# Scaling the weights instead of the activations in the opening of an attention and MLP kernel, with the warm-up dummies rearranged

## The chip, the cores and the metric

One core of one Trainium2 chip. The metric is device time in microseconds (us) per execution, the median of several executions; each comes with the core's span (first to last instruction, about 1.7 us shorter in most executions) and the mean clock that the TensorE throttle granted. The engines are named as in the profile: PE is TensorE, PEld its weight loads, DVE VectorE, ACT ScalarE, POOL GpSimd, SP SyncE, which issues DMAs.

## The reference, cut to what matters

```python
x = A_x                                                   # 2048 x 512
sa, ca, ga, sb, cb, gb = silu(c) @ w_mod, cut in six      # shift, scale, gate, twice
h = layernorm(x) * (1 + ca) + sa
q = h @ wq                                                # 32 heads of 128
x = x + ga * (softmax(q k^T / sqrt(128)) v @ wo)          # 512 keys, 8 kv heads
h = layernorm(x) * (1 + cb) + sb
x = x + gb * (relu(h @ w1) @ w2)
```

The change rests on one identity. With n = layernorm(x), h @ wq = n @ ((1 + ca) wq) + sa @ wq: the scale can go into the rows of the weights, and the shift becomes a bias per column of q.

## The kernel before

The work is cut into 128 units (4 blocks of 512 rows times 32 heads). For each unit PE makes the projection q, the scores, and the product with v; ACT takes the exponentials and evacuates q; DVE divides. The main loop is dense on PE. Before it stands an opening of 13 us that loads, normalizes and transposes the first 512 rows, makes the modulation columns modc (shift and scale, one column per 128 features), and projects q for units 0 and 1 in two halves of 256 rows. Bank 4 (QBK) holds unit 0's first half, then unit 1's second half, then the projection of unit 2.

```python
warm(7); silu_exp(5); warm(9)        # dummies 128x512; silu_exp transposes c on PE
...                                   # statistics, rstd on POOL, normalized x (xn)
ln_tposes(0, TB[0])                   # tile 0 of xn, transposed by PE into PSUM
for f in mod_cols_mm(0, QBK): f()     # 32 matmuls of one column: modc
ln_norm(2)
mod_cols_evac(0, QBK)
for tl in range(1, TPB):
    ln_tposes(tl, TB[tl // 2])
mod_half(0, 0, DVE); mod_half(0, 2, ACT); mod_half(0, 1, DVE); mod_half(0, 3, ACT)   # h out of PSUM
q_half(0, 0, CC_ORDER, QBK)           # 4 matmuls, stationary wq, moving h, 256 columns
mod_half(1, 0, DVE); mod_half(1, 2, ACT); mod_half(1, 1, DVE); mod_half(1, 3, DVE)
q_evac_half(0, 0, QBK, ACT)
q_half(1, 0, CC_ORDER, 5);  q_evac_half(1, 0, 5, ACT)
q_half(0, 1, CC_ORDER, 6);  q_evac_half(0, 1, 6, DVE)
q_half(1, 1, CC_ORDER, QBK); q_evac_half(1, 1, QBK, DVE)
...
for s in range(NU):                   # main loop
    s_mms(s, 0)
    q_mms(s + QA)                     # QA = 2: the first is unit 2's projection, into QBK
    s_mms(s, 1)
    ...
```

Each operation names the resources it reads and writes; a helper turns them into semaphore waits. Two operations that write resources of one name wait for each other even where their memory is disjoint.

Of the kernel before, what the change touches and what calls it, by code (L numbers as in the profile page):

```python
# [8 lines left out]
ACTF = mybir.ActivationFunctionType  # L9
ALU = mybir.AluOpType  # L10
AX = mybir.AxisListType
BF = mybir.dt.bfloat16
F32 = mybir.dt.float32
# [1185 lines left out]
def build_fast(nc, es, top, A_x, A_k_cache, A_v_cache, A_wq, A_wo, B_x, B_w1, B_w2, c, w_mod, out, flag):  # L1199
    P = 128  # L1200
    _, Sq, D = A_x.shape
    _, G, Sk, Dh = A_k_cache.shape
# [5 lines left out]
    QB = 512  # L1208
    NB = Sq // QB
    TPB = QB // P  # L1210
    NT = Sq // P
    DC = D // P
# [3 lines left out]
    scale = float(Dh) ** -0.5  # L1216
# [11 lines left out]
    def T(name, shape, dt=BF):  # L1228
        return es.enter_context(nc.sbuf_tensor(name, shape, dt))
# [3 lines left out]
    wq_sb = wq_t[:, :].rearrange("p (c n) -> p c n", c=DC)  # L1233
# [4 lines left out]
    hT = [T(f"hT{i}", [P, DC, QB]) for i in range(2)]  # L1238
    h2T = [T(f"h2T{i}", [P, DC, QB]) for i in range(2)]
    qT = [T(f"qT{i}", [P, QB]) for i in range(NQT)]  # L1240
    PT = [T(f"PT{i}", [P, KC, QB]) for i in range(NPT)]
# [8 lines left out]
    xn = T("xn", [P, TPB, D])  # L1250
    xnT = T("xnT", [P, TPB, DC, P])
# [4 lines left out]
    ones = T("ones", [P, P])  # L1256
# [7 lines left out]
    modc = T("modc", [P, 4 * DC], F32)  # L1264
# [5 lines left out]
    mv = T("mv", [P, NT, 2], F32)  # L1270
    rstd = T("rstd", [P, NT], F32)
    cst = T("cst", [P, 4], F32)
    rinv = T("rinv", [P, NU, TPB], F32)
    vmax = T("vmax", [P, 2, G], F32)
    chk = T("chk", [P, 12], F32)
# [6 lines left out]
    bank = [s_ps[0][:, 0, :], s_ps[0][:, 1, :], s_ps[1][:, 0, :], s_ps[1][:, 1, :], q_ps[:, :],  # L1282
            o_ps[:, 0:2, :].rearrange("p a b -> p (a b)"), o_ps[:, 2:4, :].rearrange("p a b -> p (a b)"), w_ps[:, :]]
    QBK, WBK = 4, 7

    sem = lambda name: top.enter_context(nc.semaphore(name))
    kb = KB(nc)
    PE = kb.stream("pe", sem("s_pe"))
    ACT = kb.stream("act", sem("s_act"))
    DVE = kb.stream("dve", sem("s_dve"))  # L1290
    POOL = kb.stream("pool", sem("s_pool"))
# [7 lines left out]
    def dma(out_ap, in_ap, key, reads=(), writes=(), transpose=False, eng=None):  # L1299
        k = dsem(key)  # L1300
        if transpose:
            return kb.op(SP, lambda e: e.dma_start_transpose(out_ap, in_ap), reads=reads, writes=writes, dma_sem=k)
        return kb.op(eng or SP, lambda e: e.dma_start(out_ap, in_ap), reads=reads, writes=writes, dma_sem=k)  # L1303

    RL = lambda name, n: [Res(f"{name}{i}") for i in range(n)]
    R_x, R_wq, R_wo = RL("x", NT), RL("wq", H), RL("wo", NPASS)
    R_kT, R_v, R_v1 = RL("kT", G), RL("v", G), Res("v1")
    R_hT, R_h2T = [RL(f"hT{i}_", DC) for i in range(2)], [RL(f"h2T{i}_", DC) for i in range(2)]
    R_qT, R_PT, R_o, R_oT = RL("qT", NQT), [RL(f"PT{i}_", 2) for i in range(NPT)], RL("o", NOS), RL("oT", NOT)
# [3 lines left out]
    R_b = RL("bank", 8)  # L1313
# [1 line left out]
    R_moda, R_modb, R_ga, R_gb = Res("moda"), Res("modb"), Res("ga"), Res("gb")  # L1315
    R_pr = [R_ga] + RL("pr", 2) + [R_gb]
    R_st, R_mv, R_rstd = RL("st", NT), RL("mv", NT), RL("rstd", NT)
    R_h0 = RL("h0", DC)
    R_q1 = RL("q1_", 2)
    R_cf, R_m01 = Res("cf"), Res("m01")  # L1320
    R_s3, R_eps = Res("s3"), Res("eps")
# [49 lines left out]
    def mm(out_ap, lhsT, rhs, start, stop, reads, bk, signal):  # L1371
        kb.op(PE, lambda e: e.matmul(out_ap, lhsT, rhs, start=start, stop=stop), reads=reads, group_writes=[R_b[k] for k in bk], signal=signal)  # L1372
# [4 lines left out]
    def warm(n):  # L1377
        for i in range(n):
            mm(bank[WBK], ones[:, :], ones[:, 0:1].to_broadcast([P, QB]), True, True, [R_ones], [WBK], i == n - 1)
# [11 lines left out]
    def ln_norm(t):  # L1391
        b, tl = t // TPB, t % TPB
        kb.op(DVE, lambda e: e.tensor_scalar(xn[:, tl, :], x_sb[:, t, :], mv[:, t, 0:1], rstd[:, t:t + 1], op0=ALU.subtract, op1=ALU.mult),
              reads=[R_x[t], R_mv[t], R_rstd[t]], writes=[R_xn[tl]])

    def ln_dmaT():
        dma(xnT[:, :, :, :].rearrange("p t c q -> p (t c) q"), xn[:, :, :].rearrange("p t d -> p (t d)"), "xnT", reads=R_xn, writes=[R_xnT], transpose=True)

    def ln_mod_sb(cc, dst, R_dst, which):
        o, r = (0, R_moda) if which == 1 else (2 * DC, R_modb)  # L1400
# [4 lines left out]
    def ln_tposes(tl, bks):  # L1405
        for cc in range(DC):
            bk = bks[cc]
            o = (cc % 2) * 512 + tl * P
            tpose(bank[bk].bitcast(BF)[:, o:o + P], xn[:, tl, cc * P:(cc + 1) * P], [R_xn[tl]], [bk], cc == DC - 1)

    CC_ORDER = (0, 2, 1, 3)
    QA = 2

    def silu_exp(bk):
        cT = bank[bk].bitcast(BF)[:, 0:DC]
        kb.op(PE, lambda e: e.transpose(cT, c_row[:, :], ident[0:DC, 0:DC]), reads=[R_c, R_ident], group_writes=[R_b[bk]])  # L1416
        kb.op(ACT, lambda e: e.activation(tmp[:, :], cT, ACTF.Exp, scale=-1.0), reads=[R_b[bk]], writes=[R_tmp])
        kb.op(ACT, lambda e: e.activation(c_f[:, :], cT, ACTF.Copy), reads=[R_b[bk]], writes=[R_cf])
# [6 lines left out]
    def mod_cols_mm(which, bk):  # L1425
        fs = []
        for cc in range(DC):
            for sl in (0, 1):
                for c2 in range(DC):
                    last = sl == 1 and c2 == DC - 1 and cc == DC - 1  # L1430
                    fs.append(lambda sl=sl, c2=c2, cc=cc, col=sl * DC + c2, last=last: mm(
                        bank[bk][:, col:col + 1], wm[sl][:, cc, c2 * P:(c2 + 1) * P], sc_bf[:, cc:cc + 1],
                        cc == 0 and sl == 0 and c2 == 0, last, [R_sc, wm_res(sl, cc)], [bk], last))
        return fs

    def mod_cols_evac(which, bk):
        mo, r = which * 2 * DC, (R_moda, R_modb)[which]
        kb.op(DVE, lambda e: e.tensor_tensor(modc[:, mo:mo + 2 * DC], bank[bk][:, :2 * DC], m01[:, :], op=ALU.add), reads=[R_b[bk], R_m01], writes=[r])  # L1438
# [38 lines left out]
    def q_mms(u, bk=QBK):  # L1477
        b, h = units[u]
        for i, cc in enumerate(range(DC)):
            mm(bank[bk], wq_sb[:, cc, h * Dh:(h + 1) * Dh], hT[b % 2][:, cc, :], i == 0, i == DC - 1,  # L1480
               [R_wq[h], R_hT[b % 2][cc]] + ([R_h0[cc]] if b == 0 else []), [bk], i == DC - 1)
        q_evac(u, bk)

    def q_evac(u, bk=QBK):
# [80 lines left out]
    load_wq(2, 2)  # L1565
    load_k(0)
    load_v(0)
    kb.op(POOL, lambda e: e.memset(ones[:, :], 1.0), writes=[R_ones])
    kb.op(POOL, lambda e: e.memset(cst[:, 0:1], -0.5), writes=[R_cst])
    kb.op(POOL, lambda e: e.affine_select(ident[:, :], ones[:, :], pattern=[[1, P]], compare_op=ALU.is_equal, fill=0.0,  # L1570
                                          base=0, channel_multiplier=-1), reads=[R_ones], writes=[R_ident])
# [3 lines left out]
    kb.op(POOL, lambda e: e.memset(m01[:, 0:DC], 0.0), writes=[R_m01])  # L1575
    kb.op(POOL, lambda e: e.memset(m01[:, DC:2 * DC], 1.0), writes=[R_m01])
    kb.op(ACT, lambda e: e.activation(cst[:, 2:3], cst[:, 0:1], ACTF.Exp), reads=[R_cst], writes=[Res("dummy")])
    warm(7)
    silu_exp(5)
    warm(9)  # L1580
    t3 = TPB - 1
    kb.op(ACT, lambda e: e.activation(xn[:, t3, :], x_sb[:, t3, :], ACTF.Copy, accum_out=s3[:, 0:1]), reads=[R_x[t3]], writes=[R_xn[t3], R_s3])
    kb.op(ACT, lambda e: e.activation(s3[:, 1:2], s3[:, 0:1], ACTF.Copy, scale=-1.0 / D), reads=[R_s3], writes=[R_s3])
# [6 lines left out]
    def rstd_pow(lo, hi):  # L1590
# [12 lines left out]
    ln_norm(1)  # L1603
    kb.op(POOL, lambda e: e.tensor_scalar(xn[:, t3, :], x_sb[:, t3, :], s3[:, 1:2], rstd[:, t3:t3 + 1], op0=ALU.add, op1=ALU.mult),
          reads=[R_x[t3], R_rstd[t3], R_s3], writes=[R_xn[t3]])
    TB = [[0, 0, 2, 2], [1, 1, 3, 7]]
    def q_evac_half(u, hf, bk, eng):
        src, dst = bank[bk][:, hf * HB:(hf + 1) * HB], qT[u][:, hf * HB:(hf + 1) * HB]
        w = [R_q1[u]] if hf else [R_qT[u]]
        if eng is DVE:  # L1610
            kb.op(DVE, lambda e: e.tensor_copy(dst, src), reads=[R_b[bk]], writes=w)  # L1611
        else:
            kb.op(ACT, lambda e: e.activation(dst, src, ACTF.Copy), reads=[R_b[bk]], writes=w)

    ln_tposes(0, TB[0])
    fs = mod_cols_mm(0, QBK)
    for f in fs:
        f()
    ln_norm(2)
    mod_cols_evac(0, QBK)  # L1620
    HB = QB // 2
    R_half = [R_h0, R_hT[0]]

    def mod_half(hf, cc, eng):
        bk = TB[hf][cc]
        o = (cc % 2) * 512 + hf * HB
        src, dst = bank[bk].bitcast(BF)[:, o:o + HB], hT[0][:, cc, hf * HB:(hf + 1) * HB]
        sc, sh = modc[:, DC + cc:DC + cc + 1], modc[:, cc:cc + 1]
        if eng is DVE:
            kb.op(DVE, lambda e: e.tensor_scalar(dst, src, sc, sh, op0=ALU.mult, op1=ALU.add), reads=[R_b[bk], R_moda], writes=[R_half[hf][cc]])  # L1630
        else:
            kb.op(ACT, lambda e: e.activation(dst, src, ACTF.Identity, bias=sh, scale=sc), reads=[R_b[bk], R_moda], writes=[R_half[hf][cc]])

    def q_half(u, hf, order, bk):
        for cc in order:
            mm(bank[bk][:, hf * HB:(hf + 1) * HB], wq_sb[:, cc, u * Dh:(u + 1) * Dh], hT[0][:, cc, hf * HB:(hf + 1) * HB], cc == CC_ORDER[0], cc == CC_ORDER[-1],
               [R_wq[u], R_half[hf][cc]], [bk], cc == CC_ORDER[-1])

    for tl in range(1, TPB):
        ln_tposes(tl, TB[tl // 2])  # L1640
    mod_half(0, 0, DVE)
    mod_half(0, 2, ACT)
    mod_half(0, 1, DVE)
    mod_half(0, 3, ACT)
    q_half(0, 0, CC_ORDER, QBK)
    mod_half(1, 0, DVE)
    mod_half(1, 2, ACT)
    mod_half(1, 1, DVE)
    mod_half(1, 3, DVE)
    q_evac_half(0, 0, QBK, ACT)  # L1650
    q_half(1, 0, CC_ORDER, 5)
    q_evac_half(1, 0, 5, ACT)
    q_half(0, 1, CC_ORDER, 6)
    q_evac_half(0, 1, 6, DVE)
    q_half(1, 1, CC_ORDER, QBK)
    q_evac_half(1, 1, QBK, DVE)
    load_wq(R, R)
    load_k(1)
# [234 lines left out]
```

## Time and profile before

| | before |
|---|---|
| time, median of the first three executions | 560.62 us (560.35 to 561.12) |
| span of the profiled execution (561.1 us) | 559.4 us |
| PE busy | 98% |
| start of unit 2's projection in that profile | 13.56 us |

The profiled execution was the slowest of the three.

The prediction shows the lines that carry the reading. Four more, from the timeline of DVE, belong to the part that the change rewrites (start us, length us, engine, line, operation, out<-in, count): five modulations out of PSUM, the last of them among the projections, then two evacuations back to back and nothing between them.

```profile
10.30 1.36 DVE L1630 TENSOR_SCALAR hT<-psS,modc 128x256 bf16<-128x256 bf16 x4
11.59 0.40 DVE L1630 TENSOR_SCALAR hT<-psW,modc 128x256 bf16<-128x256 bf16 x1
12.55 0.43 DVE L1611 CAST qT<-psO 128x256 bf16<-128x256 f32 x1 [0.57 <-PE psO L1372]
12.99 0.42 DVE L1611 CAST qT<-psQ 128x256 bf16<-128x256 f32 x1
```

The second evacuation ends at 13.41, and unit 2's projection, which overwrites what it read, starts 0.15 later.

### The profile page before, as it was taken

The page shows a single profiled execution, that of the slowest core. Times are in us where ns is not written, and L with a number is a line of the kernel's source. Part 1 is how long each engine was busy: PE and PEld are TensorE (multiplying, and loading weights), DVE is VectorE, ACT ScalarE, POOL GpSimd, SP SyncE. Part 2 cuts the span into 40 slices and gives each one's busy share as a digit, 9 for nine tenths or more (in the row PEclk, how much of TensorE's full clock was granted, in tenths as well). Part 3 has the DMA queues.
Part 4 walks back from the last instruction along what each step waited for, and adds up shares of the span by engine and source line. Part 5 has one row for each costly group of instructions (what it writes and reads, how often), then busy time and mean ns, then how long its engine had stood idle before and what let it go on. Part 6 is the DMA issues. An engine that isn't in the chain of part 4 may idle for free.

```text
span 559.4 us, 9666 instructions
## 1 busy us (share of the span) xinstructions
PE 550.5 (98%) x4060; PEld 315.8 (56%) x4134; DVE 253.8 (45%) x551; ACT 348.9 (62%) x453; POOL 54.7 (10%) x53
## 2 busy tenths in 40 slices
PE   8999999999999999999999999999999999999998
PEld 4665555555555555555555555555555654444444
DVE  4455555553546544335445443333354448321134
ACT  4986666666666666666666666666666644432500
POOL 3000022004410000033000000332000000000000
DMA  9897763513114144352352412111215110210001
GB/s 268 248 207 174 143 169 46 114 39 76 40 38 76 39 73 117 58 133 57 94 95 57 76 40 39 39 39 38 39 39 76 39 30 0 44 34 23 22 29 47
DMA packets 113309, 42.67 MB, mean 76 GB/s; under 512 B 93928, under 2 KB 112104, under 8 KB 113256
## 3 DMA queue, kind: packets, MB, share of 16 engines
q1 hardware_dynamic: 112024, 40.82, 34.3%
q10 hardware_dynamic: 1232, 1.15, 0.6%
q8 instruction: 33, 0.54, 0.4%
q14 instruction: 20, 0.16, 0.1%
HBM read 18.35 MB, written 2.10 MB: 37 GB/s over the span
## 4 chain that ended last, share of the span: by engine, by line
PE 98%; issue 1%; DMA 1%; DVE 0%; SPq 0%; DVEq 0%
PE psS L1372 28%; PE psO L1372 27%; PE psQ L1372 23%; PE psW L1372 20%; DMA c_row<-in_c_dram 1%; DVE qT L1611 0%; DVE hT L1630 0%; SPq L1303 0%; DVE PT L1723 0%; DVE PT L1725 0%; PE psS L1375 0%; PE psO L1416 0%; DVE modc L1438 0%; DVEq L123 0%
## 5 line engine op out<-in xcount | busy, mean ns | idle before, releaser
L1493 ACT ACTIVATE PT<-psS 128x1024 bf16<-128x1024 f32 x256 | 262.7, 1028 | 128.2 <-PE psS L1372 128.1
L1372 PE MATMUL psS<-qT,kT 128*128 128x512 bf16 x508 | 150.9, 379 | 0.5 <-DVE qT L1611 0.4
L1372 PEld LDWEIGHTS psO<-v,PT 128*128 128x128 bf16 x2048 | 126.6, 98 | 30.2
L1372 PE MATMUL psO<-v,PT 128*128 128x129 bf16 x2048 | 137.0, 220 | 0.0
L1372 PE MATMUL psQ<-hT,wq 128*128 128x512 bf16 (+1 forms) x510 | 130.5, 377 | 0.3 <-DVE hT L1630 0.2
L1503 DVE RECIPROCAL rinv<-psO 128x4 f32<-128x4 f32 x128 | 23.3, 182 | 227.2 <-PE psO L1372 227.2
L1372 PE MATMUL psW<-wo,oT 128*128 128x512 bf16 x454 | 118.1, 379 | 3.0
L1504 DVE TENSOR_TENSOR o<-psO,rinv 128x512 bf16<-128x512 f32 x128 | 88.5, 691 | 4.9 <-DVE rinv L1503 0.5
L1372 PEld LDWEIGHTS psQ<-hT,wq 128*128 128x128 bf16 x512 | 49.9, 98 | 60.3 <-issue 0.6
L1372 PEld LDWEIGHTS psS<-qT,kT 128*128 128x128 bf16 x512 | 49.5, 98 | 58.9 <-ACT PT L1493 0.7
L1485 ACT ACTIVATE qT<-psQ 128x512 bf16<-128x512 f32 x126 | 74.7, 593 | 0.0
L1712 ACT ACTIVATE wq<-psS 128x512 bf16<-128x512 f32 x56 | 33.4, 597 | 49.3 <-PE psS L1372 48.9
L1372 PEld LDWEIGHTS psW<-wo,oT 128*128 128x128 bf16 x512 | 45.0, 98 | 32.9 <-DVE acc L1526 1.2
L1526 DVE TENSOR_TENSOR acc<-psW,acc 128x512 f32<-128x512 f32 x48 | 33.2, 691 | 6.5 <-PE psW L1372 6.5
L1372 PE MATMUL psO<-wmw,wq 128*128 128x512 bf16 (+1 forms) x165 | 32.8, 352 | 0.3
L1529 POOL TENSOR_TENSOR acc<-acc,gaf 128x512 f32<-128x512 f32 x12 | 15.6, 1303 | 146.7 <-DVE acc L1526 139.8
L1388 POOL TENSOR_TENSOR rstd<-rstd,cst 128x4 f32<-128x4 f32 x7 | 7.2, 1025 | 216.8 <-DVE rstd L1387 216.8
L1723 DVE TENSOR_TENSOR PT<-psO,gbf 128x512 f32<-128x512 f32 (+1 forms) x12 | 7.5, 624 | 40.4 <-PE psO L1372 40.4
L1372 PE MATMUL psS<-h2T,wmw 128*128 128x512 bf16 x109 | 25.0, 379 | 0.2
L1372 PEld LDWEIGHTS psO<-wmw,wq 128*128 128x128 bf16 x168 | 15.3, 98 | 16.5
L1372 PE MATMUL psS<-hT,wmw 128*128 128x512 bf16 x110 | 24.4, 379 | 0.1
L1382 DVE BATCH_NORM_STATS2 st<-x 128x6 f32<-128x512 bf16 x31 | 21.1, 681 | 4.8 <-DMA x<-in_A_x_dram 4.8
(85 smaller groups left out, 192.6 us busy)
## 6 DMA issues: line engine op xcount, KB each, us to landing
wo<-in_A_wo_dram SPq DMA_DIRECT2D x4, 1024.0 KB, 5.9
wq<-in_A_wq_dram SPq DMA_DIRECT2D x7, 512.0 KB, 4.6
wmw<-in_B_w_dram SPq DMA_DIRECT2D x14, 256.0 KB, 3.1
wmw<-in_w_mod_dram SPq DMA_DIRECT2D x5, 512.0 KB, 4.8
oT<-o SPq DMA_TRANSPOSE x128, 2.4
out_dram<-PT SPq DMA_DIRECT2D x15, 128.0 KB, 1.7
x<-in_A_x_dram SPq DMA_DIRECT2D x3, 512.0 KB, 4.3
v<-in_A_v_cache_dram SPq DMA_DIRECT2D x8, 128.0 KB, 3.8
```

The lines of the kernel that those rows point to most:

```text
L1372: kb.op(PE, lambda e: e.matmul(out_ap, lhsT, rhs, start=start, stop=stop), reads=reads, group_writes=[R_b[k] for k in bk], signal=signal)
L1382: kb.op(DVE, lambda e: e.bn_stats(st[:, t, :], x_sb[:, t, :]), reads=[R_x[t]], writes=[R_st[t]])
L1388: kb.op(POOL, lambda e: e.tensor_tensor(rstd[:, sl], rstd[:, sl], cst[:, 0:1].to_broadcast([P, hi - lo]), op=ALU.pow), reads=R_rstd[sl] + ...
L1485: kb.op(ACT, lambda e: e.activation(qT[u % NQT][:, :], bank[bk], ACTF.Copy), reads=[R_b[bk]], writes=[R_qT[u % NQT]])
L1493: kb.op(ACT, lambda e: e.activation(PT[u % NPT][:, pr * 2:pr * 2 + 2, :], s_ps[pr][:, :, :], ACTF.Exp, scale=scale), reads=[R_b[pr * 2], R ...
L1503: kb.op(DVE, lambda e: e.reciprocal(rinv[:, u, :], o_ps[:, :, P]), reads=[R_b[5], R_b[6]], writes=[R_rinv])
L1504: kb.op(DVE, lambda e: e.tensor_tensor(o_sb[u % NOS][:, :, :], o_ps[:, :, 0:P], rinv[:, u, :].unsqueeze(2).to_broadcast([P, TPB, P]), op=A ...
L1526: kb.op(DVE, lambda e: e.tensor_tensor(acc[:, tl, :], bank[WBK], acc[:, tl, :], op=ALU.add), reads=[R_b[WBK], R_acc[tl]], writes=[R_acc[tl]])
L1529: kb.op(eng, lambda e: e.tensor_tensor(acc[:, tl, :], acc[:, tl, :], gaf[:, :], op=ALU.mult), reads=[R_acc[tl], R_ga], writes=[R_acc[tl]])
L1712: kb.op(ACT, lambda e: e.activation(h1T[b % 2][:, fc, :], bank[bk], ACTF.Relu), reads=[R_b[bk]], writes=[R_h1[b % 2][fc]], pre=all_events( ...
L1723: kb.op(DVE, lambda e: e.tensor_tensor(yt[i][:, c0:c1], bank[bk][:, c0:c1], gbf[:, c0:c1], op=ALU.mult), reads=[R_b[bk], R_gb], writes=[R_ ...
```

## The change

Its intent: the first projections need not wait for a modulated h. Plain normalized x is copied out of PSUM while the modulation is still being computed; modc then scales 256 weight columns; the shift enters as a bias at the evacuation of q. The dummies are rearranged so that PE has no idle time between them. h itself is still needed from unit 2 on, and is now made later, from the copied x.

```diff
-    kb.op(POOL, lambda e: e.memset(ones[:, :], 1.0), writes=[R_ones])
+    kb.op(DVE, lambda e: e.memset(ones[:, :], 1.0), writes=[R_ones])
-    warm(7)
-    silu_exp(5)
-    warm(9)
+    warm(10)
+    silu_exp(5)
+    warm(7)
...
+    wqs = PT[2][:, :, 0:2 * Dh]                            # scaled weights, in a buffer still free
+    R_wqs = [R_PT[2][cc // 2] for cc in range(DC)]
...
     ln_tposes(0, TB[0])
+    ln_tposes(1, TB[0])
     (modulation matmuls)
     ln_norm(2)
+    x_evac(0, 1, DVE, 2)                                   # plain x, PSUM to SBUF
     mod_cols_evac(0, QBK)
-    (eight mod_half, woven among the projections)
+    x_evac(0, 0, ACT, 0)
+    (transposes of tiles 2 and 3)
+    for cc in range(DC):                                   # DVE: weights times (1 + ca)
+        wqs[:, cc, :] = wq_sb[:, cc, 0:256] * modc[:, DC + cc]
+    (POOL: shift to bf16; PE: 8 one-column matmuls; ACT: qb, the bias)
+    q_half(0, 0, QBK);  q_half(1, 0, 5)
+    x_evac(1, 0, ACT, 1);  x_evac(1, 1, DVE, 3)
+    q_evac_half(0, 0, QBK, ACT);  q_evac_half(1, 0, 5, ACT)   # now adding qb
+    q_half(0, 1, 6);  q_half(1, 1, QBK)
+    h_mod(3, POOL);  h_mod(0, DVE)                         # h for units 2 and later
+    q_evac_half(0, 1, 6, DVE)
+    h_mod(1, DVE);  h_mod(2, DVE)
+    q_evac_half(1, 1, QBK, DVE)
```

(Lines in parentheses and the wqs line are shortened; cuts are marked with dots.)

More of the change, by code (lines that the diff above doesn't have):

```diff
@@ L1272, in build_fast @@
     cst = T("cst", [P, 4], F32)
+    sh_bf = T("sh_bf", [P, DC])
+    qb = T("qb", [P, 2], F32)
+    wqs = PT[2][:, :, 0:2 * Dh]
     rinv = T("rinv", [P, NU, TPB], F32)
@@ L1317, in build_fast @@
     R_st, R_mv, R_rstd = RL("st", NT), RL("mv", NT), RL("rstd", NT)
-    R_h0 = RL("h0", DC)
+    R_xh = [RL(f"xh{i}_", 2) for i in range(2)]
+    R_sh, R_qb = Res("sh"), Res("qb")
+    R_wqs = [R_PT[2][cc // 2] for cc in range(DC)]
     R_q1 = RL("q1_", 2)
@@ L1396, in ln_dmaT @@
     def ln_dmaT():
-        dma(xnT[:, :, :, :].rearrange("p t c q -> p (t c) q"), xn[:, :, :].rearrange("p t d -> p (t d)"), "xnT", reads=R_xn, writes=[R_xnT], transpose=True)
+        dma(xnT[:, :, :, :].rearrange("p t c q -> p (t c) q"), xn[:, :, :].rearrange("p t d -> p (t d)"), "xnT", reads=R_xn, writes=[R_xnT] + R_xh[0] + R_xh[1], transpose=True)
     def ln_mod_sb(cc, dst, R_dst, which):
@@ L1409, in ln_tposes @@
             tpose(bank[bk].bitcast(BF)[:, o:o + P], xn[:, tl, cc * P:(cc + 1) * P], [R_xn[tl]], [bk], cc == DC - 1)
-    CC_ORDER = (0, 2, 1, 3)
     QA = 2
@@ L1480, in q_mms @@
             mm(bank[bk], wq_sb[:, cc, h * Dh:(h + 1) * Dh], hT[b % 2][:, cc, :], i == 0, i == DC - 1,
-               [R_wq[h], R_hT[b % 2][cc]] + ([R_h0[cc]] if b == 0 else []), [bk], i == DC - 1)
+               [R_wq[h], R_hT[b % 2][cc]], [bk], i == DC - 1)
         q_evac(u, bk)
@@ L1605, in build_fast @@
           reads=[R_x[t3], R_rstd[t3], R_s3], writes=[R_xn[t3]])
-    TB = [[0, 0, 2, 2], [1, 1, 3, 7]]
+    TB = [[0, 0, 2, 2], [1, 1, 3, 3]]
     def q_evac_half(u, hf, bk, eng):
@@ L1610, in q_evac_half, with x_evac @@
         if eng is DVE:
-            kb.op(DVE, lambda e: e.tensor_copy(dst, src), reads=[R_b[bk]], writes=w)
+            kb.op(DVE, lambda e: e.tensor_scalar(dst, src, qb[:, u:u + 1], None, op0=ALU.add), reads=[R_b[bk], R_qb], writes=w)
         else:
-            kb.op(ACT, lambda e: e.activation(dst, src, ACTF.Copy), reads=[R_b[bk]], writes=w)
+            kb.op(ACT, lambda e: e.activation(dst, src, ACTF.Identity, bias=qb[:, u:u + 1]), reads=[R_b[bk], R_qb], writes=w)
+    HB = QB // 2
+    HT = TPB // 2
+    def x_evac(hf, j, eng, bk):
+        src = bank[bk].bitcast(BF).rearrange("p (c t q) -> p c t q", c=2, t=TPB)[:, :, hf * HT:(hf + 1) * HT, :]
+        dst = xnT[:, hf * HT:(hf + 1) * HT, 2 * j:2 * j + 2, :].rearrange("p t c q -> p c t q")
+        if eng is DVE:
+            kb.op(DVE, lambda e: e.tensor_copy(dst, src), reads=[R_b[bk]], writes=[R_xh[hf][j]])
+        else:
+            kb.op(ACT, lambda e: e.activation(dst, src, ACTF.Copy), reads=[R_b[bk]], writes=[R_xh[hf][j]])
     ln_tposes(0, TB[0])
+    ln_tposes(1, TB[0])
     fs = mod_cols_mm(0, QBK)
@@ L1619, in build_fast @@
     ln_norm(2)
+    x_evac(0, 1, DVE, 2)
     mod_cols_evac(0, QBK)
-    HB = QB // 2
-    R_half = [R_h0, R_hT[0]]
-    def mod_half(hf, cc, eng):
-        bk = TB[hf][cc]
-        o = (cc % 2) * 512 + hf * HB
-        src, dst = bank[bk].bitcast(BF)[:, o:o + HB], hT[0][:, cc, hf * HB:(hf + 1) * HB]
-        sc, sh = modc[:, DC + cc:DC + cc + 1], modc[:, cc:cc + 1]
-        if eng is DVE:
-            kb.op(DVE, lambda e: e.tensor_scalar(dst, src, sc, sh, op0=ALU.mult, op1=ALU.add), reads=[R_b[bk], R_moda], writes=[R_half[hf][cc]])
-        else:
-            kb.op(ACT, lambda e: e.activation(dst, src, ACTF.Identity, bias=sh, scale=sc), reads=[R_b[bk], R_moda], writes=[R_half[hf][cc]])
@@ L1634, in q_half @@
-    def q_half(u, hf, order, bk):
-        for cc in order:
-            mm(bank[bk][:, hf * HB:(hf + 1) * HB], wq_sb[:, cc, u * Dh:(u + 1) * Dh], hT[0][:, cc, hf * HB:(hf + 1) * HB], cc == CC_ORDER[0], cc == CC_ORDER[-1],
-               [R_wq[u], R_half[hf][cc]], [bk], cc == CC_ORDER[-1])
-    for tl in range(1, TPB):
-        ln_tposes(tl, TB[tl // 2])
-    mod_half(0, 0, DVE)
-    mod_half(0, 2, ACT)
-    mod_half(0, 1, DVE)
-    mod_half(0, 3, ACT)
-    q_half(0, 0, CC_ORDER, QBK)
-    mod_half(1, 0, DVE)
@@ L1647, in build_fast, with q_half @@
-    mod_half(1, 2, ACT)
-    mod_half(1, 1, DVE)
-    mod_half(1, 3, DVE)
+    x_evac(0, 0, ACT, 0)
+    def q_half(u, hf, bk):
+        for cc in range(DC):
+            mm(bank[bk][:, hf * HB:(hf + 1) * HB], wqs[:, cc, u * Dh:(u + 1) * Dh], xnT[:, hf * HT:(hf + 1) * HT, cc, :], cc == 0, cc == DC - 1,
+               [R_wqs[cc], R_xh[hf][cc // 2]], [bk], cc == DC - 1)
+    for tl in range(2, TPB):
+        ln_tposes(tl, TB[tl // 2])
+    for cc in range(DC):
+        kb.op(DVE, lambda e, cc=cc: e.tensor_scalar(wqs[:, cc, :], wq_sb[:, cc, 0:QA * Dh], modc[:, DC + cc:DC + cc + 1], None, op0=ALU.mult),
+              reads=[R_wq[0], R_wq[1], R_moda], writes=[R_wqs[cc]])
@@ new lines, in build_fast @@
+    kb.op(POOL, lambda e: e.tensor_copy(sh_bf[:, :], modc[:, 0:DC]), reads=[R_moda], writes=[R_sh])
+    for u in range(QA):
+        for cc in range(DC):
+            mm(bank[WBK][:, u:u + 1], wq_sb[:, cc, u * Dh:(u + 1) * Dh], sh_bf[:, cc:cc + 1], cc == 0, cc == DC - 1, [R_wq[u], R_sh], [WBK], u == QA - 1 and cc == DC - 1)
+    q_half(0, 0, QBK)
+    q_half(1, 0, 5)
+    x_evac(1, 0, ACT, 1)
+    x_evac(1, 1, DVE, 3)
+    kb.op(ACT, lambda e: e.activation(qb[:, :], bank[WBK][:, 0:QA], ACTF.Copy), reads=[R_b[WBK]], writes=[R_qb])
@@ L1650, in build_fast, with h_mod @@
     q_evac_half(0, 0, QBK, ACT)
-    q_half(1, 0, CC_ORDER, 5)
     q_evac_half(1, 0, 5, ACT)
-    q_half(0, 1, CC_ORDER, 6)
+    q_half(0, 1, 6)
+    q_half(1, 1, QBK)
+    def h_mod(cc, eng):
+        kb.op(eng, lambda e: e.tensor_scalar(hT[0][:, cc, :].rearrange("p (t q) -> p t q", t=TPB), xnT[:, :, cc, :], modc[:, DC + cc:DC + cc + 1],
+                                             modc[:, cc:cc + 1], op0=ALU.mult, op1=ALU.add),
+              reads=[R_xh[0][cc // 2], R_xh[1][cc // 2], R_moda], writes=[R_hT[0][cc]])
@@ L1654, in build_fast @@
+    h_mod(3, POOL)
+    h_mod(0, DVE)
     q_evac_half(0, 1, 6, DVE)
-    q_half(1, 1, CC_ORDER, QBK)
+    h_mod(1, DVE)
+    h_mod(2, DVE)
     q_evac_half(1, 1, QBK, DVE)
```

## The prediction

> **What bounds the kernel now.** I read the page first (part 1, busy time; part 4, the chain that ended last), then the chain of waits in order of time for the opening, then the timeline of the first 16 us engine by engine, and last the waits of PE alone. Of the page two lines matter:
>
> ```profile
> PE 550.5 (98%) x4060; PEld 315.8 (56%) x4134; DVE 253.8 (45%) x551; ACT 348.9 (62%) x453; POOL 54.7 (10%) x53
> PE 98%; issue 1%; DMA 1%; DVE 0%; SPq 0%; DVEq 0%
> ```
>
> PE is busy 98% of 559.4 us and carries 98% of the chain that ended last. So work removed from another engine is worth nothing once PE runs densely; only the moment at which PE starts to run densely counts, plus any hole made later. PE's own waits over the whole run are four, all in the first 14 us:
>
> ```profile
> PE psW L1372 <- POOL cst L1569: 1.0, 1, 1.0
> PE psO L1416 <- DMA c_row<-in_c_dram: 0.7, 1, 0.7
> PE psS L1372 <- DVE qT L1611: 0.4, 1, 0.4
> PE psQ L1372 <- DVE hT L1630: 0.2, 1, 0.2
> ```
>
> The change touches nothing outside this opening. Its chain reads so (start us, us, what):
>
> ```profile
> 1.24 3.66 DMA c_row<-in_c_dram
> 5.13 3.86 PE psW L1372 x9
> 8.98 0.22 PE psS L1375 x4
> 9.21 0.79 PE psQ L1372 x32
> 10.02 0.18 DVE modc L1438
> 10.30 0.42 DVE hT L1630
> 10.86 0.78 PE psQ L1372 x4
> 12.55 0.44 DVE qT L1611
> 13.34 0.38 PE psS L1372
> 13.72 0.87 PE psQ L1372 x4
> ```
>
> The nine psW matmuls are dummies; then x's transposes, the 32 modulation matmuls, the modulation columns modc, the modulated h, four half query projections, their evacuation, the first scores (a record is missing: the weight load at 13.10 puts their true start at 13.12), and from 13.56 the projection of unit 2. From there PE is dense to the end: 10.61 of 10.90 us busy from 13.10 to 24, 198.5 of 200 from 100 to 300. **The number to follow is therefore the start of unit 2's projection, 13.56 us;** what it moves by, the end moves by.
>
> [...] the dummies are 0.43 us apart (nine in 3.86) while later 128x512 matmuls are 0.215 apart (four in 0.86), the seven early dummies end near 4.05, PE idles until 4.95, and full speed comes only near 8.8, in the last dummy. [...] 128x512 from SBUF takes 0.406 us, 128x256 from PSUM 0.401. [...] The one POOL normalization (0.90 us, 8.70 to 9.60) overlaps a DVE one, so the trace shows no clear block; I keep 0.90.
>
> **The change, part by part.** Hand-offs as in the trace of before: DVE or POOL to PE 0.15 us, PE to DVE or ACT 0.04 after the matmul's end, DVE to itself 0.1 where it waits for its own result; steps of DVE 0.32 for 128x512 from SBUF (0.406 latency), by the same fixed part about 0.2 for 128x256 (0.27 latency, an estimate), 0.61 for 128x512 from PSUM (0.69 latency as L1524; less if a bf16 copy is faster).
>
> *Dummies.* Before: 7, the transpose of c, then 9. After: 10, the transpose, then 7, with the ones set by DVE instead of POOL (PE starts near 0.95 instead of 1.04). Ten cold dummies end at 0.95 + 10 x 0.427 = 5.22, while c has landed at 4.90. So the transpose of c, silu on POOL, the reciprocal square root queued behind it on POOL and the normalizations all slip by D = 5.23 - 4.94 = 0.29 us; D is 0 if the clock opens before 5.2. [...]
>
> *Front end.* The first normalized tile is ready at 7.82 + 0.41 = 8.23 + D, the second at 8.56 + D. Before, PE was in dummies until 8.82, so the gain here is real. But the change puts the second tile's transposes ahead of the modulation matmuls: these begin at 8.56 + 0.15 + 0.22 = 8.93 + D, against 9.04, run 0.8, and modc starts at 9.94 + D (before 10.02) and ends at 10.11 + D. With D = 0.29 that is 0.2 later than before.
>
> *From modc to the projections.* Removed: eight 128x256 modulations out of PSUM (five DVE, three ACT). Added ahead of the projections: four DVE scalings of weights, 128x256: from 10.22 + D, ready at 10.49, 10.68, 10.87, 11.06 + D; the bias chain (POOL copy of the shift 0.2, eight one-column matmuls at 0.025, one ACT copy 0.2), which lets PE into the projections at 10.76 + D. The fourth scaling rules: the first half projection streams its last matmul from 11.21 to 11.32 + D, the next three (4 x 0.109 each) end streaming at 11.76, 12.20 and 12.64 + D. The four evacuations of plain x are beside this: two lie before modc, and the later two (ACT done near 11.0 + D, DVE near 11.67 + D) come in time. Before, the projections streamed from 10.86 to 12.79. So weights instead of activations gain nothing here: same number of matmuls, one DVE chain of four in front of them.
>
> *After the projections.* Hidden before, because h was the product itself; new now: h for units 2 and later must still be made, one 128x512 on POOL (0.9, beside) and three on DVE, woven among the evacuations. DVE: h0; evacuation of unit 0's second half, 12.40 to 12.83 + D (before 12.55 to 12.98); h1; h2; evacuation of unit 1's second half. The first scores start at 12.98 + D, before 13.12. But unit 2's projection writes the bank that the last evacuation reads, and that one now stands behind two 128x512 operations: 12.75, 13.08, 13.41 + D, done 13.83 + D, PE on at **13.98 + D, against 13.56**. PE has two score matmuls (0.43) to fill the time from 12.98 and stands 0.57 us.
>
> Sum: +0.42 + D. ACT takes back a little (its first exponential comes earlier): the next projection waits for ACT at 15.68 + D against 15.32, so **+0.36 + D: 0.36 to 0.65 us later, about 0.6**[...].
>
> Against that stands the clock. [...] The timed runs, 560.35 to 561.12, spread by 0.77[...]. I put the mean loss of before beyond its profile at 0.3 us, and the change takes that loss away. Net: +0.6 - 0.3 = +0.3 us.
>
> **Rivals.** (a) *The clock rules*: the hole is gone, PE is warm in every run, and the change wins 0.5 to 1 us: 559.8. For it: the spread above, and "kept dense" as its stated aim. Against: the profile of before was warm by the first real matmul, and it is no faster than the other runs. (b) *DVE rules*: the weight scalings, the PSUM copies and h on one engine delay the last evacuation, as computed[...]: 561.5 to 562. For it: DVE has twelve operations between about 9.1 + D and 13.8 + D; against: its operations there are short. (c) *Hidden anyway*: the delay of unit 2 is refilled since ACT is nearly as loaded as PE in the first units (10.02 of 10.90 us busy from 13.10 to 24). Against: PE has no idle there either, so nothing refills it. It would give 560.6.
>
> **Range and chances.** 560.62 + 0.3 = 560.9. Low end 560.1, where D is 0 and the clock gains 0.8; high end 561.8, where D is 0.29, the clock gains nothing[...]. Two per cent is 11 us, and the whole opening lasts 13: 1% for faster, 98% for within 2%, 1% for slower.
>
> **What would show it.** In the changed profile: ten dummies without a hole and the transpose of c at about 5.2 (4.94 before); full-speed dummies among the last seven, then PE idle before the first transposes near 8.6; modc near 10.2; first scores near 13.2; a new wait of PE, psQ on DVE qT, of about 0.5 us just before unit 2's projection at about 14.2. Wrong would be: a projection of unit 2 before 13.6 (DVE faster than I take it, or D zero); no early full speed in the dense dummies[...]; or h3 on POOL as what PE waits for.

The forecast's sum came to +0.6 - 0.3 = +0.3 us, so 560.9, with a range of 560.1 to 561.8. Passages are cut, as marked, in which the author reasoned from rules that no trace of this case shows: when the clock opens, what a late opening would cost, and that POOL and DVE can hold each other up. No cut changes the sum. The 0.3 is the author's estimate, with only the spread of three executions, 0.77 us, beside it. The upper end, 561.8, and the 561.5 to 562 of rival (b) still contain the cut term for POOL and DVE, about 0.5 us of the upper end.

## The result, and the profile after

| | before | after |
|---|---|---|
| median | 560.46 us | 562.81 us |
| lowest to highest, 6 executions each | 560.09 to 561.12 | 562.31 to 563.14 |
| ratio, with 95% interval | | 1.0040 (1.0027 to 1.0053) |

A ratio is the mean time of one kernel's fast executions over that of the other's of the same rounds, so it is not quite the ratio of the medians. The change costs 2.3 us: same by the 2% rule, clearly slower by the interval, and outside the predicted range.

The page of the changed kernel has a row that the page of before did not have (that trace holds no clock record): PEclk, the granted clock in tenths over 40 slices of 14 us each.

```profile
PEclk8999999999999999999999999999999999999999
```

The 8 in the first slice says that the clock was cut in the opening. Stretches of 4 us show where (stretch, length, busy time and count of PE, PEld, DVE, ACT, POOL, then granted clock, DMA share and GB/s):

```profile
8.00:12.00 4.00, 3.39 (x62) 2.60 (x63) 3.28 (x11) 1.31 (x4) 2.01 (x4) 0.90 1.25 267
12.00:16.00 4.00, 3.53 (x17) 1.95 (x17) 1.60 (x5) 1.82 (x3) 0.55 (x1) 0.67 1.15 326
```

The clock record in the trace gives it exactly: opened at 4.38 us, halved at 11.20, open again at 14.62 (in a later trace, e7: 4.06, 10.89, 14.30). One warning: five of the 17 kept traces (before, e3, e5, e12, e13) hold no clock record at all, and a run without a record is listed with a clock of 1.0. A listed 1.0 alone doesn't prove that the clock stayed open; there the spacing of the matmuls has to show it. Nor does a late opening show in the listed mean: it reads 1.0 for the profiled execution of e1, whose dummies ran at 0.427 us each until the clock opened at 8.80. The chain of waits, in order of time (short steps of issue are left out here and below), shows what the halving does:

```profile
8.31 0.72 PE psS L1380 x8
9.03 0.79 PE psQ L1377 x32
9.84 0.18 DVE modc L1442
10.12 0.30 DVE PT L1647
10.44 0.49 DVE PT L1647 x2
10.96 0.30 DVE PT L1647
11.31 0.61 PE psQ L1377 x2
11.91 1.72 PE psO L1377 x8
13.66 0.48 DVE qT L1615
14.14 0.65 DVE hT L1664 x2
14.79 0.39 DVE qT L1615
15.33 1.02 PE psQ L1377 x4
```

The eight psO matmuls take 1.72 us; before they took 0.89. Ahead of them stand four weight scalings (PT) that are not back to back: the second and the fourth start only when the one before is complete. Behind them stand two h operations between the two evacuations. Unit 2's projection, the number that the prediction follows, starts at 15.33 instead of 13.56. PE's waits name the idle time after the dummies, which was not there in the profile before:

```profile
PE psS L1380 <- DVE xn L1398: 1.5, 1, 1.5
PE psQ L1377 <- DVE sc_f L1677: 0.3, 1, 0.3
```

The last line names sc_f, a tiny operation that follows the last evacuation on DVE; the evacuation, which ends at 15.18, is what PE needs.

### The profile page after: what moved, and what is told of

Read it like the earlier page. It is cut to its first block, busy times and chain, and to the rows that moved or that the text cites. A ratio compares the mean times of both kernels' runs of the same rounds, so it can differ in the third digit from the quotient of the medians.

```text
span 561.3 us, 9692 instructions
## 1 busy us (share of the span) xinstructions
PE 551.1 (98%) x4069; PEld 316.4 (56%) x4143; DVE 255.2 (45%) x556; ACT 349.0 (62%) x453; POOL 55.7 (10%) x54
## 4 chain that ended last, share of the span: by engine, by line
PE 97%; issue 1%; DVE 1%; POOL 0%; ACT 0%; DVEq 0%; POOLq 0%
PE psS L1377 28%; PE psO L1377 27%; PE psQ L1377 23%; PE psW L1377 20%; DVE PT L1647 0%; POOL tmp L1426 0%; DVE qT L1615 0%; PE psS L1380 0%; POOL rstd L1595 0%; DVE hT L1664 0%; DVE xn L1398 0%; DVE PT L1740 0%; DVE PT L1742 0%; POOL tmp L1425 0%; POOL sc_bf L1427 0%
## 5 line engine op out<-in xcount | busy, mean ns | idle before, releaser
L1377 PE MATMUL psQ<-hT,wq 128*128 128x512 bf16 x502 | 129.1, 379 | 0.4 <-DVE sc_f L1677 0.3
```

The costliest lines, as they stand in the source:

```text
L1377: kb.op(PE, lambda e: e.matmul(out_ap, lhsT, rhs, start=start, stop=stop), reads=reads, group_writes=[R_b[k] for k in bk], signal=signal)
```

## The experiments

**Theory A, the clock:** with the dense dummies the clock opened early (4.38 us in the trace of the changed kernel); they were through at 6.8 us, PE then had little to do until the projections, and the clock closed on them (11.20). That the one brought about the other is a conjecture. **Theory B, the DVE chain:** the opening is longer by its own dependencies whatever the clock does. They are not exclusive; the question is how much belongs to each. **C, late c:** ten cold dummies (0.427 us each, against 0.215 at full speed) hold back the transpose of c.

The experiments ran in four sets (e1 to e4, e5 to e8, e9 to e11, e12 to e14), each on another chip, each with executions of before beside it: 560.81, 560.75, 560.83 and 560.65 us (median). A comparison across sets is therefore one of ratios to before, or of traces.

### The kernel before once more

No edit, five timed executions, then two more looks in a later set.

> The kernel before, unchanged, to see the clock record of every execution and a second trace. Theory 'clock' (the changed kernel loses because its array clock closes again about 11.2 us into the run, after dense dummies opened it at 4.4): here the granted clock is 1.0 in all executions, and the time 560.5, ratio 1.000. Theory 'DVE chain' (the changed opening is simply a longer chain): the same, and the clock has no say. A second trace shows how much earlier than 13.56 unit 2's projection starts in a run of median time: about 12.9 if the 0.66 us between the profiled and the median run lies in the opening.

Measured: 560.70 us, ratio 0.9996, clock 1.0 in all five. The second trace has the clock opening at 8.80 and unit 2's projection at 13.55, like the first, whose late dummies are 0.43 us apart to the last. But the five spans run from 558.6 to 559.8: these traces showed the slow end, not the median.

> The kernel before, one look[...]. Both traces of it so far opened the clock at 8.8 us and started unit 2's projection at 13.56, with spans of 559.4 and 559.8, while its median span is about 558.9. Theory: in most executions the clock opens before the early dummies are through with c [...], the last dummies end near 7, the first transposes start near 8.2 and unit 2's projection near 13.0. Rival: the opening is the same in all executions and the spread lies in the tail of the run.

> The same once more: clock opened at 8.8 and projection at 13.56, or clock opened by 8.2 and projection at 13.0 to 13.2; nothing else.

Measured: 560.35 us and a span of 558.6 both times (single executions). The clock opened at 4.23 and at 6.62, and unit 2's projection started at 12.89 and 12.79. The chain of the first look:

```profile
8.14 0.40 PE psS L1375 x4
8.54 0.79 PE psQ L1372 x32
9.36 0.18 DVE modc L1438
9.64 0.42 DVE hT L1630
10.19 0.78 PE psQ L1372 x4
10.98 0.89 PE psO L1372 x8
11.89 0.44 DVE qT L1611
13.05 0.87 PE psQ L1372 x4
```

What follows: these two executions are 0.7 us ahead of the one whose profile I worked from. In the first look the nine late dummies run at full speed, end at 7.04, and the transposes start as soon as the first tile is ready instead of at 8.82. Of all 42 executions of before in the four sets the median span is 559.0, so the looks (558.6) show the fast end and the first profile (559.4) is 0.4 behind the middle; ten had a span of 559.7 or more, and three of these a mean clock of 0.997. In the second look PE's idle time between the early and the late dummies was 0.64 us (0.427 us counted for each dummy), and the clock opened at 6.62; in the run above it was 0.83 us, and the clock opened at 8.80. Two traces, from which nothing follows about when it opens.

### The dummies alone, in both directions

e2 is the changed kernel with the dummies of before; e3 is the kernel before with the dummies of the change.

```diff
 e2 (from after)                          e3 (from before)
-    warm(10)                            -    warm(7)
+    warm(7)                             +    warm(10)
     silu_exp(5)                              silu_exp(5)
-    warm(7)                             -    warm(9)
+    warm(9)                             +    warm(7)
 (ones on POOL again)                     (ones on DVE)
```

> The changed kernel with the dummies of before (7, transpose of c, 9; ones set on POOL). Theory 'clock': no closing at 11.2 in any execution, and most of the 2.35 us is gone: 560.9 to 561.3. Theory 'DVE chain': the closing was worth 0.5 us at most (executions of the changed kernel with clock 1.0 took 562.3), so 562.0 to 562.6.

> The kernel before with the dummies of the change alone (10, transpose, 7; ones set on DVE). Theory 'clock': the array is idle between the dummies and the first transposes here too, the clock closes in part of the executions (granted clock 0.996 to 0.998), and the time is 1 us or more above before. Theory 'DVE chain': within 0.4 us of before, 560.3 to 560.8, or a little faster, as the dummies end before the first transposes are ready.

Measured: e2 561.72 us, ratio 1.0019 (1.0007 to 1.0032); spans 559.5, 559.5, 560.0, 560.0, 560.9 and 561.3, the last with clock 0.996. e3 561.08 us, ratio 1.0003, clock 1.0 in all five.

What follows: on the old schedule the new dummies cost nothing that the interval shows (0.9990 to 1.0016), on the new one about 1.1 us (ratio 1.0040 against 1.0019; the intervals just overlap, but all six executions of the changed kernel took 562.31 or more, and four of the six of e2 561.74 or less). So neither theory has all of it: about half of the loss belongs to the rewritten projections, and half to the dummies together with them. The trace of e2, with an early-opening clock (4.80) like the look at before, gives the first half: unit 2's projection at 14.19 against 12.89. The e3 trace shows C: by the spacing of its dummies the clock opened late, the ten dummies ended near 5.4, and c was transposed at 5.48, though it is transposed at 4.61 to 4.98 in the traces where no dummy holds it.

### One dependency tag per scaled weight slice

The scalings of slices 0 and 1 write one resource name, and so do 2 and 3, because they borrow the tags of the buffer that they sit in. That is the wait seen in the chain above.

```diff
-    R_wqs = [R_PT[2][cc // 2] for cc in range(DC)]
+    R_wqs = RL("wqs", DC)
```

> The changed kernel with one dependency tag per scaled weight slice, so that the second and fourth scaling do not wait for the one before (each waits 0.12 us in the trace). Theory 'DVE chain': the fourth slice is ready 0.24 us earlier and the time falls by 0.2 to 0.3 us, to 562.5. Theory 'clock': no change beyond 0.1, or what the clock happens to do.

Measured: 562.16 us, ratio 1.0023 (1.0010 to 1.0036), spans 560.3 to 560.5, no execution with a closed clock. The four scalings in the changed kernel and in this one:

```profile
10.12 1.13 DVE L1647 TENSOR_SCALAR PT<-wq,modc 128x256 bf16<-128x256 bf16 x4
```

```profile
10.64 0.88 DVE L1647 TENSOR_SCALAR PT<-wq,modc 128x256 bf16<-128x256 bf16 x4
```

What follows: the false waits cost the scalings 0.25 us, as expected. From the start of modc to unit 2's projection it is now 4.08 us instead of 4.44 (in e2), 0.11 more than that; no run separates the rest. The time fell by more than that, because no execution had its clock closed, while four of six had in the changed kernel. Whether the quarter microsecond keeps the clock open or these five were lucky is not told apart; the one trace opened late, at 6.97, so it does not show an early opening that held.

### Filling PE's idle time

The changed kernel with 10 dummies behind the transpose of c instead of 7, and 3 between the last transposes and the bias matmuls.

```diff
     silu_exp(5)
-    warm(7)
+    warm(10)
...
     for tl in range(2, TPB):
         ln_tposes(tl, TB[tl // 2])
+    warm(3)
```

> The changed kernel with more dummies so that the array has no long idle time: 10, transpose of c, 10, and 3 between the last transposes and the bias matmuls. Theory 'clock' [...]: no execution under 1.0, the half projections are 0.11 us apart in all of them, and the time falls to about 562.3, the level of those executions of the changed kernel whose clock stayed at 1.0. Rival (the closing has another cause than too little work): executions at 0.996 as before, time 562.8.

Measured: 562.28 us, ratio 1.0026 (1.0013 to 1.0039), clock listed as 1.0 in all five. This trace is one without a clock record, so the matmuls have to tell: the eight that took 1.72 us in the chain of the changed kernel take here

```profile
12.22 0.89 PE psO L1377 x8
```

What follows: filling goes with an open clock. In the four kernels with these three dummies (e5, e10, e11, e14) none of 20 executions had a mean clock below 0.999; of the kernels on the new schedule without them, the changed kernel had 4 of 6, e2 1 of 6, e6 2 of 5, e7 2 of 6, and e4 and e13 none of 5 and 6: 9 of 34. That supports theory A, with two reservations. An execution without a clock record counts as open here, and one of e5 had a span of 561.3, as long as those of the changed kernel that closed. And of the four traces with fillers only e14's, which stayed open, is of a clock that opened about as early as in the two traces that closed (e7 at 4.06, the changed kernel at 4.38): its late dummies ran at full speed (eight of them and the transpose of c within the 2.33 us that PE was busy from 4 to 8). e10 and e11 opened later (6.02 and 6.84), e5 too by the spacing of its dummies. The price of the closing is small in the median: 0.5 us (ratio 1.0040 to 1.0026, which is 0.8 us by means), since c is late here (5.49; unit 2's projection at 14.80). In the traces on the new dummies there are two cases: an early clock (4.38), lost again at the projections (11.20, the changed kernel), or a late clock (6.97 in e4), and then c waits for cold dummies (5.48 in e3, 5.49 in e5). Both are slow on the new schedule.

### Taking lateness of c away

As e5, but 9 dummies ahead of c and 8 behind it.

> The changed kernel with dummies 9, transpose, 8 and 3 behind the last transposes: against the filled one (10, 10, 3: 562.28) it takes away only the lateness of c (5.05 instead of 5.48). Theory 'late c costs its own length': unit 2's projection at 14.3 instead of 14.8, time 561.7 to 561.9. Rival 'c is hidden behind the statistics of x': no change, 562.2.

Measured: 562.30 us, ratio 1.0028 (1.0015 to 1.0042), clock 1.0 in all five; spans 559.8 to 560.6, median 560.3, against 560.5 for e5. In this set the time exceeded the span by 1.7 to 2.7 us instead of the usual 1.7, so the spans say more than the times. In the trace c was transposed at 5.06 and unit 2's projection started at 14.38: 0.43 and 0.42 earlier than in e5. What follows: c's lateness passes to the projection in full length in the trace; the times do not resolve it, and by them the rival is not refuted.

### The order on DVE after the projections

e6 is e2 with the last evacuation ahead of h1 and h2. e7 also moves h1 to ACT, which is idle then, and has one tag per slice.

```diff
 e6                                       e7
-    h_mod(1, DVE)                       -    h_mod(1, DVE)
-    h_mod(2, DVE)                       -    h_mod(2, DVE)
     q_evac_half(1, 1, QBK, DVE)              q_evac_half(1, 1, QBK, DVE)
+    h_mod(1, DVE)                       +    h_mod(1, ACT)
+    h_mod(2, DVE)                       +    h_mod(2, DVE)
```

> The changed kernel with the dummies of before, and the last evacuation on DVE ahead of h1 and h2. Theory 'the last evacuation behind h1 and h2 holds unit 2's projection': its start moves from 14.18 (as with the old dummies alone) to about 13.6, its last matmul ends 0.4 earlier, the time falls by 0.4 against the old dummies alone: about 561.3. Rival 'h itself is the bound' (unit 2's projection needs h2 anyway): the start moves but the end does not, time unchanged at 561.7.

> As the last, with h1 on ACT (idle there) and one dependency tag per scaled weight slice. If the loss with the old dummies is the DVE chain alone, unit 2's projection starts at about 13.4 to 13.5 without a hole and the time is that of before, 560.6, or up to 0.2 less. If something else of the change costs time, it stays at 561 or more.

Measured: e6 562.55 us, ratio 1.0025; e7 561.73 us, ratio 1.0007 (0.9993 to 1.0022). Both are mixtures. e6's executions were 561.48 and 561.74, and then 562.55, 562.62 and 562.70, two of these with a clock of 0.996 or 0.997. e7's were 560.44, 560.59 and 561.22, and then 562.24, 562.45 and 562.62, two of them at 0.997; its trace is of a closed one (halved from 10.89 to 14.30). The trace of e6 is of an open one. DVE after the first of the two evacuations, in e2, then in e6:

```profile
12.92 0.73 DVE L1664 TENSOR_SCALAR hT<-xnT,modc 128x512 bf16<-128x512 bf16 x2
13.56 0.48 DVE L1615 TENSOR_SCALAR qT<-psQ,qb 128x256 bf16<-128x256 f32 x1
```

```profile
12.87 0.48 DVE L1615 TENSOR_SCALAR qT<-psQ,qb 128x256 bf16<-128x256 f32 x1
13.27 0.72 DVE L1664 TENSOR_SCALAR hT<-xnT,modc 128x512 bf16<-128x512 bf16 x2
```

What follows: the evacuation that guards unit 2's bank ends at 13.35 instead of 14.04, and from the start of modc to unit 2's projection it is 3.84 us instead of 4.44. Theory B is right about this wait, in the trace. The times do not confirm it: three of e6's five executions were slow, two of these with a closed clock, and even its two best (561.48, 561.74) are no better than e2's best four (561.21 to 561.74). So by the times the rival, that the end does not move, stands. e7's open executions reach the time of before, which says that the chain is then about as short; it also says how much the clock matters on this schedule, 2 us between the best and the worst execution of one kernel.

### The second tile's transposes behind the modulation matmuls

e13 is e2 with the old order there, and the DVE copy of x on ACT.

```diff
     ln_tposes(0, TB[0])
-    ln_tposes(1, TB[0])
     (modulation matmuls)
+    ln_tposes(1, TB[0])
     ln_norm(2)
-    x_evac(0, 1, DVE, 2)
     mod_cols_evac(0, QBK)
     x_evac(0, 0, ACT, 0)
+    x_evac(0, 1, ACT, 2)
```

> The changed kernel with the dummies of before, and the second tile's transposes behind the 32 modulation matmuls as before (with the DVE copy of x moved to ACT). Theory 'the earlier transposes delay modc by 0.4 us in a usual execution': modc at 9.3 to 9.4 instead of 9.74, unit 2's projection at 13.8 instead of 14.18, time 0.3 to 0.4 below the old dummies alone (ratio 1.001 to 1.0015 after 1.0019). Rival 'the copies of x on ACT or the transposes then come late': projection at 14.1 or later.

Measured: 561.91 us, ratio 1.0019, as e2. In the profiled execution the clock opened late (dummies until 9.11), so its trace cannot be laid beside that of e2, and the three best executions (561.30 to 561.62) are no better than e2's (561.21 to 561.70). From modc to unit 2's projection it has 4.43 us, as e2 has 4.44, so copies that come late, the rival, don't show in it. Inconclusive otherwise: no gain from this order alone is shown.

### All mends together, and two more openings

e10 has 9 and 8 dummies, the three fillers, one tag per slice, and e7's order. e14 has the same with 8 and 8 dummies, ones on POOL, and e13's order.

> The changed kernel with all four mends: dummies 9, transpose of c, 8; 3 dummies behind the last transposes; one tag per scaled weight slice; last evacuation first and h1 on ACT. Theory (clock, late c and DVE chain are all of the loss): no execution below clock 1.0, projection of unit 2 at about 13.2 to 13.5, time 560.4 to 560.8, ratio to before 0.999 to 1.000. If it stays above 561.3 something else of the change costs time.

> The changed kernel with all mends: dummies 8, transpose, 8, and 3 behind the last transposes; modulation matmuls first; one tag per weight slice; last evacuation first and h1 on ACT. Theory: projection of unit 2 at about 13.0 to 13.1, without closing of the clock; time 560.5 to 560.8, ratio 0.9995 to 1.0005: all of the loss is accounted for, but nothing is won against before. If it stays above 561.2, a part of the loss is not understood.

Measured: e10 561.28 us, ratio 1.0013 (0.9999 to 1.0026), spans 559.2 to 560.5, unit 2's projection at 13.64; e14 560.81 us, ratio 1.0000 (0.9987 to 1.0013), spans 558.9 to 559.1, unit 2's projection at 13.32. Both started that projection later than expected, and e10's time missed its range. The chain of e14, without the first scores:

```profile
8.10 0.40 PE psS L1380 x4
8.49 0.78 PE psQ L1377 x32
9.27 0.78 PE psS L1380 x12
10.11 0.78 PE psW L1377 x10
10.88 0.46 PE psQ L1377 x4
11.34 0.89 PE psO L1377 x8
12.26 0.49 DVE qT L1615
13.48 0.87 PE psQ L1377 x4
```

What follows: with all of them undone the loss is gone within the interval. The change, mended, equals before and does not beat it: in this trace unit 2's projection starts at 13.32, still 0.4 behind the first look at before. That the means are equal all the same would come from the absence of slow executions, which five executions suggest and don't show. The scalings are no longer in this chain: it runs over PE alone, and the psW line is dummies of the filling and the bias matmuls. So the fillers now stand in front of the projections themselves, and the mends without them were not run. The old order of the transposes does win in the front: modc starts 4.55 us after c's transpose, as in before, against 4.88 in e10. But unit 2's projection starts 8.56 after it, against 8.58 in e10, so behind the fillers the gain is lost again.

The last two kernels apply the finding to the kernel before: less idle time between the dummies, c not held back. e8 has dummies 9 and 8 with ones on DVE, e12 8 and 8 with nothing else changed.

```diff
 e12 (from before)
-    warm(7)
+    warm(8)
     silu_exp(5)
-    warm(9)
+    warm(8)
```

> The kernel before with dummies 9, transpose, 8 and the ones set on DVE: no hole, and c's transpose not later than its landing (1.1 + 9 x 0.427 = 4.94). Theory 'the dummies ended too late and too cold': first transposes at 8.3 instead of 8.8, unit 2's projection up to 0.5 earlier, time 560.2 or less and less spread. Rival: the array closes or opens late as elsewhere, time 560.5 to 561.

> The kernel before with dummies 8, transpose of c, 8 (7 and 9 before). Theory [...]: the hole shrinks to 0.2 to 0.45 us, c is not delayed, the clock opens by 8, unit 2's projection starts at 12.8 to 13.0 in all executions; spans 558.6 to 558.9 without the 559.4 to 559.9 of before, median time 560.4, ratio 0.999. Rival (the hole has no part in it): spread and median as before, 560.8.

Measured: e8 560.92 us, ratio 0.9998, spans 559.0 to 559.3, projection at 13.15 (c at 5.06, a little late): not the 560.2 expected, but inside the range of the rival. e12 560.46 us, ratio 0.9996 (0.9983 to 1.0009), spans 558.4 to 559.1, projection at 12.85. Against before e12 is the same: none of its five executions was slow, where two or more of ten usually are, but five executions do not show that.

## Why the prediction was wrong

**What held.** The start of unit 2's projection sets the end to a few tenths: 12.89 and a span of 558.6, 14.19 and 560.0, 14.80 and 560.5, 15.33 and 561.3. In the 17 traces the span is 545.7 to 546.4 us longer than that start. Weights in place of activations gain nothing (from modc to unit 2's projection 3.70 us in e10, with both false waits and the late evacuation gone, 3.54 in before); the four scalings are a chain in front of the projections; the last evacuation behind h1 and h2 holds unit 2. h3 on POOL (0.86 us) was beside, and rival (c), a delay refilled later, did not happen.

**What failed, first: the clock term.** The prediction put it: "I put the mean loss of before beyond its profile at 0.3 us, and the change takes that loss away." Both halves are wrong. The executions of before are on the whole *faster* than the profile that I started from: 0.4 us by the median span of 42, 0.8 in the two looks, in which the clock opened before the late dummies were through. The three times on hand hinted at it, as the profiled execution was the slowest (561.12); I worked out +0.6 against it and added it to the median, 560.62. With the dense dummies the clock did open early in the trace of the changed kernel (4.38), but I never asked whether it would stay open. In the profiled execution it was halved at 11.20, over the half projections, and cost 1.05 us where I had a gain of 0.3. Rival (a) was therefore wrong in sign, and my range too let the clock at worst gain nothing, never lose.

**Second: the size of the DVE chain.** I took 0.50 us more than before from modc to unit 2's projection (9.94 to 13.98 against 10.02 to 13.56). Measured with an open clock: 4.44 us in e2 against 3.54 in the look at before, 0.90 more. The term left out is the pair of false waits between scalings, 0.25 us on DVE (0.36 with what followed in e4), which the dependency listing of the changed kernel showed and I did not cost. My estimate for a scaling itself was right (0.286 us long, in 128x256); that of the copies of x was too long (0.42 from PSUM, not 0.69), without effect. The evacuations with a bias take 0.48 us, not 0.43.

**Third: D.** Ten cold dummies end at 5.4, not 5.22, because PE starts at 1.11 with ones on DVE, later than with POOL (1.04), not at 0.95. So D is 0.67 us with a late clock (5.48 against 4.81 in the first look at before), not 0.29. With an early one it is 0.16 (4.97), which lies within what c's own transfer varies by (4.61 to 4.98).

**Fourth: the front end.** modc comes 0.33 us later, beyond D, because the modulation matmuls wait for the second tile. Against the slow profile of before this looked like a small gain; against a fast execution it is a loss.

Added up on the profiled execution of the changed kernel against that look: c 0.16, front end 0.33, DVE chain 0.90, closed clock 1.05 (5.49 us from modc to the projection, against 4.44 in e2): 2.44 us, which is the difference of the two starts, 15.33 - 12.89. The split between chain and clock rests on e2 as the open-clock case; for the single parts of the chain it rests on traces, not on times, and a quarter of a microsecond more or less is not resolved by the medians. The traces do repeat, though, once c's varying arrival is taken out by counting from the transpose of c:

| traces | schedule | from c's transpose to unit 2's projection |
|---|---|---|
| e3, e8, e9, e9b, e12 | old | 8.08 to 8.11 us |
| e2, e5, e11 | new, clock open | 9.31 to 9.32 |
| e4 | new, one tag per slice | 8.95 |
| e6 | new, last evacuation first | 8.89 |
| e10, e14 | new, all mends | 8.58, 8.56 |
| the changed kernel | new, clock halved | 10.36 |

So the longer chain, 1.2 us (front end and DVE), stands on eight traces on four chips and not on one pair; the closed clock's 1.05 stands on one trace. (Left out: before, e1 and e13, whose late cold dummies still hold the transposes at 8.8 to 8.9, and e7, closed and mended at once, 9.71.) What exactly makes the clock close stays open. In the 3.41 us before it was halved PE idled for 0.72 us in the changed kernel (7.79 to 11.20) and for 0.79 in e7 (7.48 to 10.89); in stretches of the same length, over which the clock stayed open, it idled for 0.68 us in the first look at before (7.64 to 11.06) and for 0.30 in e2 (8.22 to 11.63). So in these four traces the idle time does not tell the two cases apart. Of the half projections' matmuls of 256 columns PE had done two and three in the first two stretches, seven and six in the others; no run tests whether that is the reason.

## What to carry to other kernels

Before you predict a change of a microsecond, look at several traces of the kernel before: here the clock opened at 4.23, 6.62 and 8.80 us in three executions of one kernel, and the one profile at hand was of a late one. Dummies that finish sooner are not a gain in themselves (here they were through at 6.8 us and the clock was halved at 11.20); follow the granted clock up to the first dense stretch. And when work is moved off the path, look at what its remainder now stands in front of: here two short h operations ahead of the evacuation that frees a bank, and a shared tag that made independent scalings wait.
